# Recurrent attention and two expert layers: one matrix-engine visit per later attention unit, new planner costs and due times, weights converted in pairs

## The chip, the cores and the metric

The kernel runs on one core of one Trainium2 chip. The metric is the device time of one launch in microseconds: 944.38 us as the median of three runs (943.25 to 944.75). One further run was profiled.

## What is computed

The reference applies a linear recurrence to r, k, v, w (4 batches, 8 heads, 768 tokens, 48 dimensions a head) and puts its output, 3072 tokens of 384 values, through two layers of two products each:

```python
for t in range(S):                                   # per batch and head
    cur = einsum('bhd,bhe->bhde', u[None] * kt, vt)
    y[:, :, t] = einsum('bhd,bhde->bhe', rt, state + cur)
    state = wt[:, :, :, None] * state + einsum('bhd,bhe->bhde', kt, vt)
h = x @ w_in                                         # 384 x 2048
x = (max(h, 0) + alpha * min(h, 0)) @ w_out          # 2048 x 384
h = x @ w_in2
out = (h * clip(h + 3, 0, 6) / 6) @ w_out2
```

## The kernel before

**Attention units.** The tokens are cut into 12 thirds of 256 tokens (three a batch); each has four pairs of heads. One third and one pair is a unit: 48 units, n = 0 to 47, each of two chunks of 128 tokens. The decay products come from two scans on DVE (`scan_t`, L386, from the back; `scan_g`, L402, from the front), between them a floor (L394) and a reciprocal (L399) on two columns. `scaled` (L423) multiplies k and r by these factors and writes `kr`, on DVE or POOL. On PE a unit then has three pieces:

- `pa` (L477, L484): k times r into bank A, and transposes of k into the same bank;
- `kv` (L516, L520): the products of the transposed k (`kT`, copied by ACT, L509) with v, into the second half of bank A, from which DVE makes the state (`Y`, L560, L562) and ACT its scaled copy (`sbd`, L538);
- `pc` (L588 to L599): the output y from state and from X, the masked `pa` (ACT writes its diagonal, L458, from a sum over the token products of L332 and L339; DVE copies the triangle in, L499).

ACT and DVE split y into a high and a low part of reduced format (L635, L641). For the fourth pair of a third they go by six small DMAs into the rows where the layers expect them (L651).

**Slots.** A layer is computed for blocks of 512 tokens (j = 0 to 5) and pieces of 128 hidden channels (f = 0 to 15): slot s = 96 m + 16 j + f for layer m. In a slot PE makes `h` (nine matmuls of 128x512, three for each of three input pieces: high by high, high by low, low by high, L765 to L767), ACT and DVE make the gate (`q` L801 or L803, `pg` L808 or L812) and split it into `g` (high L818, low L821, DVE or POOL), and PE adds nine more matmuls into three accumulators, `acc`. Blocks 0 to 5 need the outputs of units 8j to 8j+7, so units run ahead of slots; from unit 8 on they stand between slots.

**Weights** come as 64-bit numbers and are converted on the chip, one (f, part) of 128x384 at a time: ACT takes bits (`rest`, L95), DVE joins them and sets the sign (L98, L103), ACT writes the high part (L738), DVE or POOL the low one (L742). All 32 of layer 0 are made while the first 16 slots run, those of layer 1 in the slots around 96.

**Order.** Each step is given to `Plan` with its durations by engine (`where`), a due time in slots, what it needs and which buffers it takes. `Plan.run` replays this on paper: again and again it takes the engine that can start first, on it the ready step of the lowest due time, and where two engines can do a step, the one that comes first. DVE steps marked `pair` and all POOL steps exclude each other on paper. The order that comes out is written into the program, so on the chip every engine works through its list as it stands. While no `h` has begun, idle time of PE on paper is filled with small `warm` matmuls (L682).

**Checks.** Range checks (`fall`, `sum_w`, `chw` are their columns) run beside all this and set a flag at the end; by it the program goes on to a general path or not. The trace holds no instruction of that path.

**Visits.** From unit 16 on (`FUSE`), PE does `pc` of unit n-1 and `kv` of unit n in one step: `add_output` is put into `waiting` and is called when `kv` of the next unit is planned. `pa` of unit n is a step of its own.

## Time and profile before

| | |
|---|---|
| median of three runs | 944.38 us |
| profiled run, time | 943.6 us |
| profiled run, span from first to last instruction | 941.8 us |
| PE busy | 920.7 us (98%) |
| PE weight loads busy | 744.6 us (79%) |
| DVE busy | 557.1 us (59%) |
| ACT busy | 532.2 us (57%) |
| POOL busy | 133.8 us (14%) |
| granted TensorE clock, mean | 0.995 |

Busy time counts an engine from the start of an instruction to its end. On PE matmuls overlap, so that a row of 0.39 us follows the row ahead of it after 0.23 us: what a matmul costs is read from start to start, and the same goes for short instructions in a row on DVE. Times below are microseconds from the start of the span. Lines are those of the kernel before.

### The profile page before, as it was taken

The page shows a single profiled execution, that of the slowest core. Times are in us where ns is not written, and L with a number is a line of the kernel's source. Part 1 is how long each engine was busy: PE and PEld are TensorE (multiplying, and loading weights), DVE is VectorE, ACT ScalarE, POOL GpSimd, SP SyncE. Part 2 cuts the span into 40 slices and gives each one's busy share as a digit, 9 for nine tenths or more (in the row PEclk, how much of TensorE's full clock was granted, in tenths as well). Part 3 has the DMA queues.
Part 4 walks back from the last instruction along what each step waited for, and adds up shares of the span by engine and source line. Part 5 has one row for each costly group of instructions (what it writes and reads, how often), then busy time and mean ns, then how long its engine had stood idle before and what let it go on. Part 6 is the DMA issues. An engine that isn't in the chain of part 4 may idle for free.

```text
span 941.8 us, 13747 instructions
## 1 busy us (share of the span) xinstructions
PE 920.7 (98%) x4914; PEld 744.6 (79%) x4914; DVE 557.1 (59%) x1087; ACT 532.2 (57%) x1267; POOL 133.8 (14%) x132
## 2 busy tenths in 40 slices
PE   7899999999999999999999999999999999999997
PEld 5677777887888788878888888888888888888885
DVE  8999997555655645564369897353353443443432
ACT  5888777555655655565368886363353353443331
POOL 4333244021111201100012130000000000000000
PEclk9999999999999999999999999999999999999999
DMA  8888314122321320110056630060150330410001
GB/s 249 245 263 280 100 55 145 55 66 72 116 67 55 103 64 31 55 64 9 9 174 194 185 118 1 1 201 1 29 173 1 96 106 1 155 47 1 34 1 37
DMA packets 36750, 86.20 MB, mean 92 GB/s; under 512 B 5056, under 2 KB 7488, under 8 KB 36672
## 3 DMA queue, kind: packets, MB, share of 16 engines
q1 hardware_dynamic: 36240, 84.44, 28.5%
q8 instruction: 41, 0.67, 0.3%
q10 hardware_dynamic: 432, 0.79, 0.2%
q14 instruction: 37, 0.30, 0.1%
HBM read 73.41 MB, written 9.44 MB: 88 GB/s over the span
## 4 chain that ended last, share of the span: by engine, by line
PE 85%; DVE 4%; issue 2%; ACT 1%; POOL 1%; DVEq 0%; POOLq 0%; ACTq 0%
PE acc L765 14%; PE acc L766 13%; PE acc L767 13%; PE h L765 13%; PE h L767 13%; PE h L766 13%; PE A L477 2%; PE y L595 2%; PE y L588 1%; PE A L484 1%; DVE wb L98 1%; DVE wb L103 1%; DVE w L742 1%; DVE pg L808 0%; POOL kr L423 0%
## 5 line engine op out<-in xcount | busy, mean ns | idle before, releaser
L765 PE MATMUL acc<-g,w 128*128 128x512 f32 x576 | 228.9, 397 | 0.0
L767 PE MATMUL acc<-g,w 128*128 128x512 f32 x576 | 224.6, 390 | 0.0
L766 PE MATMUL acc<-g,w 128*128 128x512 f32 x576 | 224.4, 390 | 0.0
L818 ACT ACTIVATE g<-pg 128x512 fp32r<-128x512 f32 x192 | 120.7, 629 | 139.6 <-PE acc L767 126.6
L821 DVE TENSOR_TENSOR g<-pg,g 128x512 fp32r<-128x512 f32 x176 | 122.4, 696 | 124.6 <-ACT g L818 124.3
L765 PEld LDWEIGHTS acc<-g,w 128*128 128x128 f32 x576 | 108.1, 188 | 23.4 <-issue 0.4
L767 PEld LDWEIGHTS acc<-g,w 128*128 128x128 f32 x576 | 108.1, 188 | 22.8
L766 PEld LDWEIGHTS acc<-g,w 128*128 128x128 f32 x576 | 108.2, 188 | 21.2
L812 DVE SCALAR_TENSOR_TENSOR pg<-q,h 128x512 f32<-128x512 f32 x96 | 65.9, 687 | 99.6 <-ACT q L803 99.4
L803 ACT ACTIVATE q<-h,three 128x512 f32<-128x512 f32 x96 | 65.7, 685 | 101.9 <-PE h L767 101.7
L808 DVE SCALAR_TENSOR_TENSOR pg<-h,q 128x512 f32<-128x512 f32 x96 | 66.0, 688 | 96.1 <-ACT q L801 96.1
L765 PE MATMUL h<-xt,w 128*128 128x512 f32 x288 | 116.1, 403 | 0.8 <-ACT w L738 0.7
L767 PE MATMUL h<-xt,w 128*128 128x512 f32 x288 | 113.0, 392 | 0.7 <-DVE w L742 0.7
L766 PE MATMUL h<-xt,w 128*128 128x512 f32 x288 | 112.2, 390 | 0.0
L765 PE MATMUL h<-x,w 128*128 128x512 f32 x288 | 112.0, 389 | 0.0
L766 PE MATMUL h<-x,w 128*128 128x512 f32 x288 | 112.0, 389 | 0.0
L767 PE MATMUL h<-x,w 128*128 128x512 f32 x288 | 112.0, 389 | 0.0
L801 ACT ACTIVATE q<-h,nal 128x512 f32<-128x512 f32 x96 | 65.5, 683 | 74.0 <-PE h L767 71.8
L423 POOL TENSOR_TENSOR kr<-un,tg 112x512 f32<-112x512 f32 (+1 forms) x43 | 46.4, 1080 | 230.2 <-PE y L588 207.0
L767 PEld LDWEIGHTS h<-xt,w 128*128 128x128 f32 x288 | 54.1, 188 | 13.9 <-DVE w L742 2.0
L765 PEld LDWEIGHTS h<-xt,w 128*128 128x128 f32 x288 | 54.9, 191 | 12.4 <-ACT w L738 1.4
L765 PEld LDWEIGHTS h<-x,w 128*128 128x128 f32 x288 | 54.1, 188 | 11.3
(95 smaller groups left out, 1264.8 us busy)
## 6 DMA issues: line engine op xcount, KB each, us to landing
wraw<-in_w SPq DMA_DIRECT2D x64, 384.0 KB, 4.1
un<-in_unit SPq DMA_DIRECT2D x48, 337.3 KB, 3.2
raw<-in_w SPq DMA_DIRECT2D x32, 384.0 KB, 3.9
rk<-in_tok SPq DMA_DIRECT2D x24, 384.0 KB, 3.8
v<-in_vch SPq DMA_DIRECT2D x12, 384.0 KB, 3.1
x2d<-st SPq DMA_DIRECT2D x18, 256.0 KB, 2.1
x2r<-x2d SPq DMA_DIRECT2D x18, 256.0 KB, 4.7
out<-st SPq DMA_DIRECT2D x15, 256.0 KB, 4.5
```

Of the source, the lines that this page charges most:

```text
L423: eng[e].tensor_tensor(out=u["kr"][:, i].rearrange("p a (c s) -> p a c s", c=2), in0=u["in"][:, 0 : 2 * TH].rearrange("p (a c s) -> p a c ...
L477: nc.tensor.matmul(A[h][:, cs], kr[r0 : r0 + D, 0, cs], kr[r0 : r0 + D, 1, cs], start=True, stop=True,)
L595: nc.tensor.matmul(y[0:m0, cs], v[:, c, c0 : c0 + m0], X[:, c, :], start=False, stop=True, skip_group_check=True,)
L765: nc.tensor.matmul(ps, whi, xhi, start=start, stop=False, skip_group_check=True)
L766: nc.tensor.matmul(ps, whi, xlo, start=False, stop=False, skip_group_check=True)
L767: nc.tensor.matmul(ps, wlo, xhi, start=False, stop=stop, skip_group_check=True)
L801: nc.scalar.activation(q, k["h"], AF.Relu, scale=nal[:, f : f + 1])
L803: nc.scalar.activation(q, k["h"], AF.Relu, bias=three)
L808: nc.vector.scalar_tensor_tensor(out=p, in0=k["h"], scalar=0.0, in1=k["q"], op0=ALU.max, op1=ALU.subtract)
L812: nc.vector.scalar_tensor_tensor(out=p, in0=k["q"], scalar=6.0, in1=k["h"], op0=ALU.min, op1=ALU.mult)
L818: nc.scalar.activation(k["g"][:, 0], k["p"], AF.Copy)
L821: eng[e].tensor_tensor(out=k["g"][:, 1], in0=k["p"], in1=k["g"][:, 0].bitcast(F32), op=ALU.subtract)
```

## The change

Six things change together.

1. For units 16 to 47 (`late`) one PE step, `add_visit`, does `pc` of unit n-1, `kv` of unit n and `pa` of unit n+1. KV moves from bank A into the second half of y's bank. `triangle` waits for `pa` and no longer for `kv`. `kT` has one buffer and `kr` three (two before).
2. The floor is gone: the reciprocal reads the scan's column, and ACT copies that column for the check at the end (`keep`). There is one `gfirst`, not two.
3. Weights are converted in groups (f, 0) and (f-2, 1): 14 pairs and four single ones for each layer. A pair is loaded by two DMAs, and `rest`, `join`, sign, high and low each work on 768 columns. The low part of a pair is on DVE alone.
4. The planner gets new durations for nearly every step, waits by engine, a model of SP's queue, and of two engines that can start at the same moment takes the one that could have started first by itself (`asked`), which bears on POOL and DVE.
5. A table, `URGENCY`, shifts due times of 23 kinds of steps in four ranges of due time up to slot 95, and ties some kinds to one engine: token products (`weigh_tokens`) and the halves of `kr` of the first units (`scale_half`) to POOL in the first range, the low part of g (`add_slot.glo`) to DVE up to slot 80.
6. `v` buffers take the place of `wv` for the range check of weights.

Of the table some lines, and the planner's constants, where they are read, and the choice between engines:

```diff
+URGENCY = {
...
+    "add_slot.glo": {1: (0, "DVE"), 2: (0, "DVE")},
+    "add_slot.h_": {1: (-3.0, None), 2: (1.0, None), 3: (-1.0, None)},
...
+    "scale_half": {0: (0, "POOL")},
+    "second": {2: (-0.5, None), 3: (2.0, None)},
+    "state1": {1: (7.5, None)},
+    "weigh_tokens": {0: (0, "POOL"), 1: (1.0, "DVE"), 2: (0, "DVE")},
...
-    LATENCY = 0.08
-    SAME = {"PE": 0.0, "DVE": 0.1, "ACT": 0.15, "POOL": 0.1, "SP": 0.0}
-    SPARE = 0.46
-    COLD = 9.5
-    LOCK = True
-    BEGIN = {"PE": 1.2, "DVE": 2.0, "ACT": 2.0, "POOL": 3.0, "SP": 0.6}
+
+    TAIL = {"PE": 0.0, "DVE": 0.08, "ACT": 0.1, "POOL": 0.04, "SP": 0.0}
+    LATENCY = {"PE": 0.26, "DVE": 0.06, "ACT": 0.05, "POOL": 0.08, "SP": 0.0}
+    SAME = {"PE": 0.0, "DVE": 0.02, "ACT": 0.02, "POOL": 0.02, "SP": 0.0}
+    STAGES = (-0.5, 16, 80, 95)
+    ISSUE, FLIGHT = 0.45, 1.6
+    SPARE = 0
+    COLD = 8.0
+    BEGIN = {"PE": 1.4, "DVE": 3.1, "ACT": 5.2, "POOL": 3.0, "SP": 0.7}
```

```diff
+        kind = kind or fn.__qualname__.replace("<locals>.", "").split(".", 1)[1]
+        if due < self.STAGES[-1]:
+            stage = sum(due >= x for x in self.STAGES)
+            shift, engine = URGENCY.get(kind, {}).get(stage, (0.0, None))
+            due += shift
+            if engine and len(where) > 1:
+                where = {engine: where[engine]}
```

```diff
             for e, lst in ready.items():
                 if lst:
                     t = min(earliest(e, o) for o in lst)
-                    if best is None or t < best[0]:
-                        best = (t, e)
+                    o = min((o for o in lst if earliest(e, o) <= t), key=lambda o: rank(e, o))
+                    asked = max(free[e], o["t"][e])
+                    if best is None or (t, asked) < best[:2]:
+                        best = (t, asked, e, o)
```

```diff
+            t, _, e, o = best
...
             o["eng"], o["start"], o["end"] = e, t, t + d
-            free[e] = t + d
-            if self.LOCK and (e == "POOL" or (e == "DVE" and o["pair"])):
-                pair = t + d
+            free[e] = t + d - self.TAIL[e]
+            if e == "POOL" or (e == "DVE" and o["pair"]):
+                pair = free[e]
             if e == "SP":
-                o["end"] = t + d + 2.0
+                queue = o["end"] = max(t + self.ISSUE + self.FLIGHT, queue) + d
+                free[e] = max(t + self.ISSUE, queue - self.FLIGHT - d)
             if not (o.get("filler") and self.started):
```

Units: the floor and its columns, then `pa` and `kv`:

```diff
-        def floor(e):
-            nc.vector.tensor_scalar(
-                fall[0:PR, n], u["T"][:, :, 0], 2.0**-60, None, op0=ALU.max
-            )
-
         def recip(e):
-            nc.vector.reciprocal(first_g[:, :, 0], fall[0:PR, n])
+            nc.vector.reciprocal(first_g[:, :, 0], u["T"][:, :, 0])
+
+        def keep(e):
+            nc.scalar.activation(fall[0:PR, n], u["T"][:, :, 0], AF.Copy)
...
-        first_g = gfirst[n % 2]
-        gb = plan.buf("gfirst", 2)
-        o_t = plan.op({"DVE": 0.34}, d - 3.7, scan_t, [o_load], new=[tgb], use=[ub_], pair=True)
-        o_f = plan.op({"DVE": 0.07}, d - 2.4, floor, [o_t], use=[tgb])
-        o_d1 = plan.op({"DVE": 0.08}, d - 2, recip, [o_f], new=[gb])
+        first_g = gfirst
+        gb = plan.buf("gfirst", 1)
+        o_t = plan.op({"DVE": 0.69}, d - 3.7, scan_t, [o_load], new=[tgb], use=[ub_], pair=True)
+        o_d1 = plan.op({"DVE": 0.16}, d - 2.4, recip, [o_t], new=[gb], use=[tgb])
+        plan.op({"ACT": 0.2}, d + 2, keep, [o_t], use=[tgb])
         o_g = plan.op(
-            {"DVE": 0.34}, d - 1.5, scan_g, [o_d1], use=[tgb, ub_, gb], pair=True
+            {"DVE": 0.69}, d - 1.5, scan_g, [o_d1], use=[tgb, ub_, gb], pair=True
```

```diff
-        o_pa = plan.op({"PE": 0.89 + 0.1 * nkv}, d - 2, pa, o_kr, new=abufs, use=[krb])
+        pa_us = 0.73 + 0.1 * nkv
+        if waiting:
+            o_pa = waiting.pop()(pa_us, pa, o_kr, abufs, [krb])
+        else:
+            o_pa = plan.op({"PE": pa_us}, d - 2, pa, o_kr, new=abufs, use=[krb])
...
-        ktb = plan.buf("kT", 2)
+        ktb = plan.buf("kT", 1)
...
+        kv_after = [o_kt, v_op[t][0]]
+        if late:
+            o_tri = plan.op({"DVE": 0.73}, d - 1.5, triangle, [o_pa, o_x], use=abufs + [xb])
         else:
-            o_kv = plan.op({"PE": 0.1 + 0.13 * nkv}, d + 0.4, kv, kv_after, use=kv_use)
-        o_tri = plan.op({"DVE": 0.61}, d - 1.5, triangle, [o_kv, o_x], use=abufs + [xb])
```

```diff
+        def add_visit(more=0.0, then=None, after=(), new=(), use=()):
+
+
+            yb = plan.buf("y", 1)
+            last_pc, last_us, last_need, last_use, last_out = u["prev"]
+
+            def run(e):
+                bank = room(e)
+                if last_pc:
+                    last_pc(e, bank)
+                u["KV"] = bank[:, 1, 0 : 2 * D].rearrange("p (c e) -> p c e", c=2)
+                kv(e)
+                if then:
+                    then(e)
+
+            o = plan.op(
+                {"PE": last_us + 0.13 * nkv + more}, d + 0.4, run,
+                kv_after + last_need + list(after), new=[yb] + list(new),
+                use=[ktb, vb] + last_use + list(use), kind="visit",
+            )
+            add_states(o, [yb])
+            if last_out:
+                last_out(o, yb)
+            ended.append((pc, pc_us, need, [krb, xb, vb] + sb, add_output))
+            return o
...
+        if late:
+            u["prev"] = ended.pop()
+            if n + 1 < NU:
+                waiting.append(add_visit)
+            else:
+                add_visit()
+                ended.pop()
+                add_end()
         else:
-            add_output()
+            add_states(o_kv, abufs)
```

Weights:

```diff
         def load(e):
-            k["raw"] = wp.tile([P, DM], w1.dtype, tag=tag, name=f"wraw{name}")
-            nc.sync.dma_start(k["raw"], (w1, w2)[m][f, part])
+            k["raw"] = wp.tile([P, n, DM], w1.dtype, tag=tag, name=f"wraw{name}")
+            for i, (m, f, part) in enumerate(keys):
+                nc.sync.dma_start(k["raw"][:, i], (w1, w2)[m][f, part])
...
+        o_l = plan.op({"SP": 1.26 * n}, due - 4, load, new=[wb])
+        o = plan.op({"ACT": 0.18 + 0.45 * n}, due - 0.2, rest, [o_l], new=[ab, bb], use=[wb])
         for i in (1, 2):
             o = plan.op(
-                {"DVE": 0.47}, due - 2, lambda e, i=i: k["steps"][i](), [o], use=[wb, ab, bb],
-                pair=True,
-            )
-        read = [add_range(key, due, o_l, [wb], lambda: k["raw"])] if m else []
-        o = plan.op({"ACT": 0.42}, due - 2.5, hi, [o] + read, use=[wb, bb])
-        w_ops[key] = plan.op(
-            {"POOL": 0.96, "DVE": 0.47}, due - 1, lo, [o], use=[bb, wb], pair=True
-        )
+                {"DVE": 0.15 + 0.4 * n}, due - 2, lambda e, i=i: k["steps"][i](), [o],
+                use=[wb, ab, bb], pair=True,
+                kind="join",
+            )
...
+        o = plan.op({"ACT": 0.21 + 0.31 * n}, due - 2.5, hi, [o] + read, use=[wb, bb])
+        where = {"POOL": 1.05, "DVE": 0.55} if n == 1 else {"DVE": 0.15 + 0.4 * n}
+        o = plan.op(where, due - 1, lo, [o], use=[bb, wb], pair=True)
...
-    for s, part, f in halves:
-        add_weight((0, f, part), s + W0)
+    for s in range(NF + 2):
+        add_weights([(0, f, part) for s1, part, f in halves if s1 == s], s + W0)
```

**PE, slots 39 to 41.** y, A and kr with a number are tiles of that unit, h and g of that slot; first before, the visit with the output of unit 29 and KV of unit 30 behind h of slot 40:

```order
L599 MATMUL y29_3143<-X29_2967,v7_2551 48x128
L516 MATMUL A30_3091<-v7_2551,kT30_3114 64x48
L520 MATMUL A30_3091<-v7_2551,kT30_3114 48x48
L516 MATMUL A30_3091<-v7_2551,kT30_3114 64x48
L520 MATMUL A30_3091<-v7_2551,kT30_3114 48x48
L765 MATMUL acc0_2_0_2856<-g38_3043,w0_6_1_1323 128x512
```

Further down in the same list, behind nine acc matmuls, comes `pa` of unit 31:

```order
L766 MATMUL acc0_2_2_2878<-g38_3043,w0_6_1_1323 128x512
L767 MATMUL acc0_2_2_2878<-g38_3043,w0_6_1_1323 128x512
L477 MATMUL A31_3188<-kr31_3162 128x128 x4
L484 MATMUL A31_3188<-ident_90,kr31_3162 128x112 x2
L765 MATMUL h42_3206<-xt2_1846,w0_10_0_1457 128x512
L766 MATMUL h42_3206<-xt2_1846,w0_10_0_1457 128x512
```

After, the same place (KV of unit 30 goes into y30 here):

```order
L651 MATMUL y30_3119<-X29_2962,v7_2533 48x128
L655 MATMUL y30_3119<-X29_2962,v7_2533 48x128
L565 MATMUL y30_3119<-v7_2533,kT30_3048 64x48
L569 MATMUL y30_3119<-v7_2533,kT30_3048 48x48
L565 MATMUL y30_3119<-v7_2533,kT30_3048 64x48
L569 MATMUL y30_3119<-v7_2533,kT30_3048 48x48
L519 MATMUL A31_3130<-kr31_3082 128x128 x4
L527 MATMUL A31_3130<-ident_93,kr31_3082 128x112 x2
L871 MATMUL acc0_2_0_2772<-g39_3095,w0_9_0_1372 128x512
L872 MATMUL acc0_2_0_2772<-g39_3095,w0_9_0_1372 128x512
L873 MATMUL acc0_2_0_2772<-g39_3095,w0_9_0_1372 128x512
L871 MATMUL h41_3150<-xt2_1905,w0_9_0_1372 128x512
```

`pa` of unit 31 has moved from between acc and h to right behind `kv` of unit 30, and the acc matmuls of slot 39 now stand around h of slot 41, two slots behind their own.

**DVE, weights of f = 6 in the first layer** (wb is joined, then signed; w its low part; tg a scan). Before:

```order
L808 SCALAR_TENSOR_TENSOR pg4_1156<-h4_1037,q4_1069 128x512
L98 SCALAR_TENSOR_TENSOR wb0_6_0_1120<-wraw0_6_0_888,wa1_107 128x384
L98 SCALAR_TENSOR_TENSOR wb0_4_1_1151<-wraw0_4_1_909,wa0_106 128x384
L103 SCALAR_TENSOR_TENSOR wb0_6_0_1120<-wraw0_6_0_888,wb0_6_0_1120 128x384
L103 SCALAR_TENSOR_TENSOR wb0_4_1_1151<-wraw0_4_1_909,wb0_4_1_1151 128x384
L386 SCALAR_TENSOR_TENSOR tg0_111<-un14_1008,restart_108 112x258
L402 SCALAR_TENSOR_TENSOR tg1_112<-un13_922,gfirst1_110 112x258
L742 TENSOR_TENSOR w0_6_0_1178<-wb0_6_0_1120,w0_6_0_1178 128x384
L742 TENSOR_TENSOR w0_4_1_1182<-wb0_4_1_1151,w0_4_1_1182 128x384
```

After:

```order
L98 SCALAR_TENSOR_TENSOR wb0_6_0_1118<-wraw0_6_0_667,wa0_109 128x768
L928 TENSOR_TENSOR g2_1157<-pg2_1135,g2_1157 128x512
L103 SCALAR_TENSOR_TENSOR wb0_6_0_1118<-wraw0_6_0_667,wb0_6_0_1118 128x768
L430 SCALAR_TENSOR_TENSOR tg0_113<-un14_1070,restart_111 112x258
L438 RECIPROCAL gfirst_112<-tg1_114 112x2
L915 SCALAR_TENSOR_TENSOR pg3_1191<-h3_1050,q3_1079 128x512
L843 TENSOR_TENSOR w0_6_0_1182<-wb0_6_0_1118,w0_6_0_1182 128x2x384
L444 SCALAR_TENSOR_TENSOR tg1_114<-un13_989,gfirst_112 112x258
L98 SCALAR_TENSOR_TENSOR wb0_7_0_1133<-wraw0_7_0_920,wa0_109 128x768
```

Two instructions of 384 columns became one of 768, and the low part of g stands on DVE between them.

**POOL, first units** (kr halves of 112x256, rk the token products). Before:

```order
L423 TENSOR_TENSOR kr0_167<-un0_142,tg_0_162 112x256
L332 TENSOR_TENSOR rk1_158<-rk1_158 128x384
L423 TENSOR_TENSOR kr1_221<-un1_181,tg_1_209 112x256 x2
L423 TENSOR_TENSOR kr2_271<-un2_197,tg_2_239 112x256
L423 TENSOR_TENSOR kr3_298<-un3_200,tg_3_262 112x256
L332 TENSOR_TENSOR rk2_207<-rk2_207,u_sb_95 128x384
L332 TENSOR_TENSOR rk3_229<-rk3_229,u_sb_95 128x384
L296 TENSOR_SCALAR nal_96<-alp_61 128x16
```

After:

```order
L465 TENSOR_TENSOR kr0_170<-un0_143,tg_0_164 112x256 x2
L375 TENSOR_TENSOR rk0_153<-rk0_153 128x384
L375 TENSOR_TENSOR rk0_153<-rk0_153,u_sb_98 128x384
L375 TENSOR_TENSOR rk1_173<-rk1_173 128x384
L375 TENSOR_TENSOR rk1_173<-rk1_173,u_sb_98 128x384
L465 TENSOR_TENSOR kr1_255<-un1_179,tg_1_219 112x256 x2
L465 TENSOR_TENSOR kr2_303<-un2_190,tg_2_269 112x256 x2
L338 TENSOR_SCALAR nal_99<-alp_61 128x16
L465 TENSOR_TENSOR kr3_340<-un3_217,tg_3_324 112x256
```

All four products of a third, and both halves of `kr`, are now POOL's.

## Rows read from the trace of the kernel before

**Rows 1.** The page: span and count of instructions

```profile
span 941.8 us, 13747 instructions
```

**Rows 2.** Windows: us, then busy us (instructions) of each engine, clock, DMA

```profile
0.00:55.58 55.58, 44.60 (x419) 33.34 (x420) 50.07 (x130) 41.35 (x139) 22.20 (x36) 0.94 0.79 234
55.58:141.10 85.52, 82.59 (x477) 62.52 (x478) 83.77 (x173) 69.57 (x182) 27.67 (x21) 1.00 0.56 176
150.73:941.80 791.07, 784.89 (x3959) 642.08 (x3958) 414.76 (x769) 413.47 (x927) 79.41 (x71) 1.00 0.23 72
```

**Rows 3.** Waits of PE, 150.73 to the end: heading, and no row under it

```profile
engine line waited for: us in total, times, longest us
```

**Rows 4.** Waits of PE over the span: us, times, longest; one of ten rows

```profile
PE A L477 <- DVE fall L394: 1.0, 1, 1.0
```

**Rows 5.** Timeline of DVE: start us, us, instruction; gate of the sixteenth slot

```profile
140.43 0.68 DVE L808 SCALAR_TENSOR_TENSOR pg<-h,q 128x512 f32<-128x512 f32 x1
```

**Rows 6.** Timeline of PE: first h matmul, and a steady pair of slots

```profile
55.58 0.47 PE L765 MATMUL h<-xt,w 128*128 128x512 f32 x1
...
154.94 0.39 PE L765 MATMUL h<-xt,w 128*128 128x512 f32 x1
...
156.98 0.60 PE L588 MATMUL y<-kr,sbd 112*112 112x128 f32 x4
...
157.99 0.21 PE L516 MATMUL A<-v,kT 128*64 128x48 f32 x1
...
158.30 0.50 PE L765 MATMUL acc<-g,w 128*128 128x512 f32 x1
...
160.57 0.71 PE L477 MATMUL A<-kr 48*128 48x128 f32 x8
...
161.30 0.47 PE L765 MATMUL h<-xt,w 128*128 128x512 f32 x1
...
163.47 0.39 PE L765 MATMUL acc<-g,w 128*128 128x512 f32 x1
```

**Rows 7.** Timeline of PE: kv, then pa, in the first stretch

```profile
32.65 0.21 PE L516 MATMUL A<-v,kT 128*64 128x48 f32 x1
...
32.96 0.71 PE L477 MATMUL A<-kr 48*128 48x128 f32 x8
```

**Rows 8.** Timeline of DVE: consecutive instructions, for the prices

```profile
134.45 0.68 DVE L808 SCALAR_TENSOR_TENSOR pg<-h,q 128x512 f32<-128x512 f32 x1
135.06 0.15 DVE L399 RECIPROCAL gfirst<-fall 112x2 f32<-112x2 f32 x1
135.13 1.00 DVE L98 SCALAR_TENSOR_TENSOR wb<-wraw,wa 128x384 int32<-128x384 int32 x2
136.05 1.01 DVE L103 SCALAR_TENSOR_TENSOR wb<-wraw,wb 128x384 int32<-128x384 int32 x2
136.99 0.68 DVE L402 TENSOR_TENSOR_SCAN tg<-un,gfirst 112x258 f32<-112x258 f32 x1
137.60 0.66 DVE L821 TENSOR_TENSOR g<-pg,g 128x512 fp32r<-128x512 f32 x1
138.18 0.25 DVE L562 SCALAR_TENSOR_TENSOR Y<-Y,tg,A 112x48 f32<-112x48 f32 x1
```

**Rows 9.** Timeline of POOL, then of DVE: one POOL product and the floor

```profile
4.99 0.64 POOL L423 TENSOR_TENSOR kr<-un,tg 112x256 f32<-112x256 f32 x1 [1.93 <-DVE tg L386]
7.92 0.99 POOL L332 TENSOR_TENSOR rk<-rk 128x384 f32<-128x384 f32 x1 [2.30 <-DMA rk<-in_tok]
...
84.74 1.29 POOL L332 TENSOR_TENSOR rk<-rk 128x384 f32<-128x384 f32 x1 [7.09 <-DMA rk<-in_tok]
...
85.05 1.00 DVE L394 TENSOR_SCALAR fall<-tg 112x2 f32<-112x2 f32 x1
```

**Rows 10.** Timeline of PE, then DVE: end of h, low half of g

```profile
303.86 0.40 PE L767 MATMUL h<-xt,w 128*128 128x512 f32 x1
...
308.67 0.67 DVE L821 TENSOR_TENSOR g<-pg,g 128x512 fp32r<-128x512 f32 x1
```

266 lines of the change are left out of this document (155 added, 111 removed).

## The prediction

> **What bounds the kernel now.** I read the windows first, then the waits of PE, then PE's own order of time. The span of 941.8 us [rows 1] falls into three stretches [rows 2]: before the first `h` matmul at 55.58 us [rows 6], from there to 141.1, and the rest. In the last stretch (150.73 to the end, 791 us) the list of PE's waits is empty [rows 3]: PE alone sets its length, DVE is busy for 415 of 791 us, and whatever is to be gained there must be time of PE itself. The middle stretch is another matter. DVE is busy for 83.8 of 85.5 us [rows 2], and PE's longest wait behind it is for a DVE instruction [rows 4]. The gate of the sixteenth slot (the last `pg` that needs a first-layer weight to be new) ends at 141.1 [rows 5]; DVE was busy for 50.1 + 83.8 = 133.9 us up to it. So up to slot 16 DVE's queue decides, behind it PE's.
>
> PE in a steady pair of slots [rows 6]: an undisturbed block of nine matmuls takes 156.98 - 154.94 = 2.04 us, 0.227 each. The visit "output of unit n-1, then KV of unit n" takes 158.30 - 156.98 = 1.32; the acc block behind it and ahead of the next visit takes 160.57 - 158.30 = 2.27; `pa` takes 0.73, and the h block behind it 163.47 - 161.30 = 2.17. So the way out of `pa` costs 0.13, and the acc block's 0.23 is the way out of one visit and the way into the next; I split it into halves.
>
> **The change, part by part.** *One visit, not two.* The matmuls stay the same: `pc`, `kv` and `pa` now stand in a row, and one way in and one way out go. Of 0.23 + 0.13 = 0.36 a unit the joined visit keeps one way out, 0.13; saved is 0.23 us, if going from `kv` to `pa` costs nothing of its own. The trace has that pair in the first stretch: `kv` starts at 32.65 and `pa` at 32.96 [rows 7], 0.31 us for eight passes, the same as from `kv` to `acc` (157.99 to 158.30). The longest stretch holds 28 `pa` visits (of 48 units; one stands about every 10.4 us until 444 us), and all 28 are now behind a `kv`: 28 x 0.23 = **6.4 us**. Bounds: 28 x 0.12 = 3.4 if the way into `pa` (0.11) stays, 31 x 0.23 = 7.1 if three earlier units count too. No cover is needed, since PE waits for nothing there; what is late next is PE again.
>
> What the rule of the tiling page makes of it: the Trainium skill, TensorEngine Tiling (Array Packing), section Key Properties, says that changing the tiling mode, not just the tile, drains the TensorE. `kv` and `pa` split the array differently, so by that rule the way from one to the other would be paid inside the visit too, and the saving would be 3.4 and not 6.4. The 0.31 us of the early pair speaks against a charge on top of the one that every exit from `kv` pays.
>
> Moved with it: the KV tile lies in the output's bank, so the copies of state wait for the whole visit, and `triangle` waits for `pa` alone. `pa` of unit n+1 comes a fraction of a slot earlier than its own visit did; its `kr` on POOL must be ready, or output and KV behind it in PE's queue wait too. POOL is busy for 79 of 791 us in this stretch [rows 2], so I cost this at nothing; if the cover failed, each 0.1 us would cost 3 us over the units.
>
> *Up to slot 16: DVE's work.* Prices are start to start from consecutive instructions [rows 8]: a 2-element op 0.07 (reciprocal at 135.06, next at 135.13), a 512-element op 0.61 and 0.58 (at 134.45 and 137.60), a 384-element op 0.46 (two from 135.13 to 136.05), a scan 0.61. A 768-element op is in no row: it lies between 0.61 and two of 0.46, and the line through 0.46 and 0.595 gives 0.46 + 3 x 0.135 = 0.87 as an estimate, which I take; a 256-element op by the same line 0.33. Counted in the order of DVE up to the sixteenth gate, before against after: join and sign 64 x 0.46 = 29.4 against 28 x 0.87 + 8 x 0.46 = 28.0, so -1.4; low halves of weights 22 x 0.46 against 14 x 0.87, +2.1 (eight fewer on POOL); low halves of g 8 against 15, +4.2 (none on POOL now); `kr` 7 whole and 5 halves against 1 whole, -5.3; floors 19 against none, -1.3; scans 38 against 36, -1.2; one token product and one memset less, -0.8; state, triangle and output copies that now come later, -1.9. Sum: **-5.6 us**. Pairing thus gives little; the rest is work moved.
>
> *The port.* An op on POOL stops DVE: the product at 84.74 took POOL 1.29, and the floor, a 2-element op, that DVE started at 85.05 ended only at 86.05, after 1.00 us [rows 9]. In the first 141 us POOL is busy for 22.2 + 27.7 = 49.9 us [rows 2], and DVE for 133.9; counted with the prices above DVE's work is some 117, so about 17 us are stretch, a third of a us for each of POOL. After, POOL has 6 to 12 us less to do by that place (41 against 43 products, the 512-element ones of `g` gone, more of the cheap half `kr`). That is -2 to -4 us; I take -2.8.
>
> So the sixteenth gate ends at 141.1 - 5.6 - 2.8 = 132.7. Not all of 8.4 is a gain: in the new order PE has by then one slot of acc matmuls (2.04) and one unit (about 2.4) fewer behind it: 8.4 - 4.5 = 3.9. The stall of 1.0 behind it [rows 4] should go as well: 5. Upper bound: all of PE's stall. Between 55.58 and 150.73 PE has 33 blocks of 2.04, nine `pa` and eight or nine of the other visit at the prices above (18.1, with 3.1 for entries), 88.5 of 95.15, so 6.7 us are stall; and DVE's work before the first gate is 5.1 us less by the same prices (ten token products and `kr` pieces are POOL's now), so the first `h` can come up to 5.1 earlier: 11.8 together. Lower bound: nothing, see the second rival. I take **7.0 us**, near the 5 of the DVE sum, and above it because the planner's durations now stand near the rows (scan 0.69, low half of `kr` on POOL 0.64), so that fewer DVE instructions should stand in line behind a POOL one.
>
> *The rest.* The weights of a pair come by two DMAs in a row, the same bytes, with the DMA engines 56% busy in the middle stretch [rows 2]: nothing. Between the last output of block 1 and the `h` that needs it stand 27 matmuls, `kv` and `pa`, 7.3 us, for output copies and six small DMAs; if these took longer, PE would wait once, a us or so, at slot 16 alone (in later blocks slots stand between): nothing in the sum. `keep` puts a 2-element copy per unit on ACT, which has half its time free behind 150 us and is not what the sixteenth gate waits for: nothing, or at worst 0.2 x 17 units = 3 us of ACT in the crowded stretch. The second layer's weights are made between 480 and 600 us; PE did not wait for them [rows 3], and DVE's work there changes by about +3 us (POOL's low halves) with POOL's stretch gone: nothing. The last store is untouched.
>
> **Sum.** The profiled run took 943.6 us for a span of 941.8, and the median of the three is 944.38, 0.8 above it. 6.4 + 7.0 = 13.4 less: span 928.4, run 930.2, against the median **931.0 us**.
>
> **Rivals.** *The start gains nothing (0.15).* POOL takes all token products and `kr` halves before the first `h`: 33 products instead of 22 up to `kr` of unit 11, about 26 us instead of 17 at 0.64 and 0.99 for a half `kr` and a product [rows 9]. If the port is what decides, those 9 us eat the 5.1 of DVE and the gate comes no earlier. For it: rows 9; against: in the first stretch POOL was busy for only 22 of 55.6 us. Then 944.4 - 6.4 = 938.0. The Trainium skill, SBUF — State Buffer, section Who interferes with whom, has the rule behind this: a DVE instruction with two SBUF inputs and a GpSimd one that reads SBUF exclude each other for the whole instruction. The stretched floor agrees.
>
> *The way into `pa` is still paid (0.10).* 6.4 becomes 3.4: 934.0.
>
> *DVE stops being the bound at once (0.12).* All 11.8 us come: 944.4 - 6.4 - 11.8 = 926.2, or 925.5 with 31 units.
>
> *Slower: second-layer input too late (0.05).* In the new order the acc matmuls of a slot begin two slots after its `h` block in slots 16 to 80, not three: between the end of `h` and the first acc stand one visit (2.2 us) and 24 matmuls (5.4 us), 7.6 us in all. A `g` took 303.86 + 0.40 = 304.26 to 308.67 + 0.67 = 309.34, 5.1 us [rows 10]. Up to 7.6 nothing is lost; beyond it each us costs 1 us in each of 32 pairs. At 8.05 us the 13.4 are gone; at 8.5 they are overdrawn, 931 + 32 x 0.9 = 960. Against it: DVE and ACT are about half busy there.
>
> *The joined visit does not arise (0.02):* the order shows that it does. The same time within 1.9 us, 0.2% (what a measurement of this kernel can tell from no change), would need both gains to fail.
>
> **How the numbers follow.** Forecast 0.56: 931, between 926 and 936. With the rivals: start without gain 0.15 at 938, way in paid 0.10 at 934, full gain 0.12 at 926, slower 0.05, same 0.02. For 8 in 10 the range is 924.5 to 938.5. Faster 0.93, same 0.02, slower 0.05.
>
> **What would show it.** Right: from slot 20 to 80 one visit a unit, 0.31 us from `kv` to `pa`, no second 2.17 us block, and PE's wait list empty from the seventeenth slot on; the sixteenth gate near 133 us; DVE still above 90% up to there. Wrong: `pa` starting later than 0.31 us behind `kv`; the first `h` behind 56 us with POOL back to back (second rival's sign); waits of acc blocks for `g` between 150 and 470 us.

## The result, and the profile after

| | before | changed |
|---|---|---|
| median of six runs each | 943.82 us | 935.32 us (933.76 to 939.31) |
| ratio | | 0.9914 (95%: 0.9895 to 0.9934) |
| profiled run, span | 941.8 us | 937.5 us |
| first `h` | 55.58 | 55.97 |
| gate of the sixteenth slot ends | 141.1 | 135.63 |

The kernel became 8.5 us faster by the medians; 13.4 had been forecast (931.0 us). The profiled run of the changed kernel is the slowest of its six (939.31), so its trace shows less of a gain than the medians do; below a second profile of it stands beside this one. Lines are those of the kernel whose trace is shown; the experiments' lines may be shifted by a few.

The page of the changed kernel: span, then busy us, share and instructions of each engine.

```profile
span 937.5 us, 13798 instructions
...
PE 919.5 (98%) x4999; PEld 753.4 (80%) x4999; DVE 553.0 (59%) x957; ACT 528.8 (56%) x1260; POOL 139.2 (15%) x128
```

Windows of the changed kernel (us, then busy us and instructions of PE, PEld, DVE, ACT and POOL, granted clock, DMA share, GB/s): up to the first `h`, from there to the sixteenth gate, and 2.5 us close behind a wait that is told of below.

```profile
0.00:55.97 55.97, 49.98 (x508) 39.00 (x509) 45.63 (x103) 43.27 (x153) 31.58 (x47) 1.00 0.82 241
55.97:135.63 79.66, 77.07 (x441) 58.72 (x439) 76.76 (x128) 62.59 (x142) 11.20 (x9) 1.00 0.55 176
151.97:154.51 2.54, 2.54 (x7) 1.97 (x6) 2.47 (x6) 1.84 (x6) 0.04 (x1) 0.51 0.01 3
```

These answer to [rows 2]. Up to the sixteenth gate DVE is now busy for 45.6 + 76.8 = 122.4 us, against 133.9 before, and POOL for 42.8 against 49.9. DVE's list got 11.5 us lighter, and the gate only 5.5 us earlier: DVE stood idle for 13.2 us on the way, against 7.3. The gate's row, on DVE:

```profile
134.94 0.69 DVE L915 SCALAR_TENSOR_TENSOR pg<-h,q 128x512 f32<-128x512 f32 x1
```

Waits of PE over the whole span (us, times, longest):

```profile
engine line waited for: us in total, times, longest us
PE acc L872 <- DVE g L928: 2.5, 1, 2.5
PE A L519 <- POOL kr L465: 2.2, 2, 1.2
PE h L871 <- DVE pg L915: 2.0, 2, 1.7
PE warm L772 <- POOL ident L318: 1.4, 1, 1.4
PE y L644 <- ACT sbd L589: 1.0, 2, 0.7
PE A L565 <- ACT kT L558: 1.0, 2, 0.5
PE y L651 <- DVE X L548: 0.7, 1, 0.7
```

None of them lies behind 160 us. The largest is new: PE waits for a low half of `g`, once, for 2.5 us.

A steady visit, timeline of PE: `pc` (y from kr and sbd), `kv` (y from v), `pa` (A from kr), then h and acc.

```profile
163.57 0.60 PE L644 MATMUL y<-kr,sbd 112*112 112x128 f32 x4
...
164.58 0.21 PE L565 MATMUL y<-v,kT 128*64 128x48 f32 x1
...
164.89 0.72 PE L519 MATMUL A<-kr 48*128 48x128 f32 x8
...
165.62 0.47 PE L871 MATMUL h<-xt,w 128*128 128x512 f32 x1
...
167.75 0.39 PE L871 MATMUL acc<-g,w 128*128 128x512 f32 x1
```

`kv` to `pa` is 164.89 - 164.58 = 0.31 us, as in [rows 7]. The h block behind the visit takes 167.75 - 165.62 = 2.13, where before two blocks a unit were over 2.04, with 2.27 and 2.17 [rows 6].

**One table for all runs.** The work of PE from slot 24 to slot 80, and from there to the end, is the same in every kernel here, and PE waits for nothing in it (but for one 0.46 us in `pa_apart`). So each trace splits at two places: the start of `h` of slot 24 and of slot 80. In all but `before`, `visits_alone`, `no_table` and `only_glo`, PE has done 12 acc matmuls more by slot 24 (22 1/3 blocks, not 21); 12 x 0.227 = 2.72 us are taken off there and added behind. The two rows of PE, before, then changed (186.08 - 2.72 = 183.36):

```profile
182.16 0.48 PE L765 MATMUL h<-xt,w 128*128 128x512 f32 x1
...
472.02 0.39 PE L765 MATMUL h<-xt,w 128*128 128x512 f32 x1
```

```profile
186.08 0.39 PE L871 MATMUL h<-xt,w 128*128 128x512 f32 x1
...
466.92 0.39 PE L871 MATMUL h<-xt,w 128*128 128x512 f32 x1
```

| kernel | median, us | first h | h of slot 24 | from there to slot 80 |
|---|---|---|---|---|
| before | 943.8 to 944.7 | 55.58 | 182.16 | 289.86 |
| changed | 935.32 | 55.97 | 183.36 | 283.56 |
| changed, second profile | 936.51 | 54.58 | 179.56 | 283.56 |
| visits_alone | 940.39 | 54.37 | 184.15 | 284.17 |
| pa_apart | 940.30 | 52.71 | 177.28 | 290.17 |
| rk_slow | 932.36 | 56.80 | 180.83 | 283.56 |
| flight4 | 933.26 | 58.09 | 177.85 | 283.56 |
| load_late | 939.46 | 54.05 | 184.67 | 283.56 |
| rk_scale | 936.38 | 55.48 | 182.19 | 283.56 |
| single_dve | 936.43 | 52.01 | 180.43 | 283.56 |
| rk_scan | 937.12 | 56.04 | 181.65 | 283.56 |
| dma_more | 937.26 | 56.67 | 181.15 | 283.55 |
| no_table | 944.06 | 52.24 | 188.57 | 283.56 |
| only_glo | 940.36 | 52.85 | 186.25 | 283.56 |

Read it by columns. The last one has two values: about 290 with two visits a unit, about 283.6 with one. Between the two slots stand 25 `pa` visits in the kernel before and none of its own in the changed one; this gains 289.86 - 283.56 = 6.30 us, 0.25 each (5.7 us in `visits_alone`). All else is the column of slot 24, which comes from one execution each (those times move by up to 4 us between executions of one kernel), and the medians. In the changed kernel's first profile the start lost 1.2 us, and the last store landed 0.8 us later behind its last matmul: 6.3 - 1.2 - 0.8 = 4.3, the difference of the two spans. Medians of two changed kernels are compared with care: each stands beside its own runs of the kernel before, each ratio is known to some 2 us either way, and the changed kernel itself gave 935.32 and 936.51. Differences of 3 to 5 us between two of them are at the edge of what this tells, and their sizes are rough.

### The profile page after: what moved, and what is told of

Its sections match the earlier page's. It is cut to its first block, busy times and chain, and to the rows that moved or that the text cites. A ratio compares the mean times of both kernels' runs of the same rounds, so it can differ in the third digit from the quotient of the medians.

```text
span 937.5 us, 13798 instructions
## 1 busy us (share of the span) xinstructions
PE 919.5 (98%) x4999; PEld 753.4 (80%) x4999; DVE 553.0 (59%) x957; ACT 528.8 (56%) x1260; POOL 139.2 (15%) x128
## 4 chain that ended last, share of the span: by engine, by line
PE 90%; DVE 3%; DMA 2%; ACT 2%; issue 1%; POOL 0%; SPq 0%; ACTq 0%; DVEq 0%; POOLq 0%
PE acc L871 14%; PE h L871 14%; PE acc L872 14%; PE acc L873 14%; PE h L873 13%; PE h L872 13%; PE A L519 3%; PE y L651 2%; DMA un<-in_unit 2%; PE y L644 2%; PE A L527 1%; DMA rk<-in_tok 1%; DVE tg L444 1%; ACT wa L95 1%; PE y L655 1%
## 5 line engine op out<-in xcount | busy, mean ns | idle before, releaser
L928 DVE TENSOR_TENSOR g<-pg,g 128x512 fp32r<-128x512 f32 x162 | 112.6, 696 | 116.5 <-ACT g L925 114.8
L465 POOL TENSOR_TENSOR kr<-un,tg 112x512 f32<-112x512 f32 (+1 forms) x55 | 55.6, 1012 | 344.9 <-DVE tg L444 266.9
L871 PEld LDWEIGHTS h<-xt,w 128*128 128x128 f32 x288 | 54.5, 189 | 15.4 <-issue 2.9
L873 PEld LDWEIGHTS h<-xt,w 128*128 128x128 f32 x288 | 54.4, 189 | 11.5
L872 PEld LDWEIGHTS h<-xt,w 128*128 128x128 f32 x288 | 54.4, 189 | 11.3
```

Source lines behind the costliest of these rows:

```text
L465: eng[e].tensor_tensor(out=u["kr"][:, i].rearrange("p a (c s) -> p a c s", c=2), in0=u["in"][:, 0 : 2 * TH].rearrange("p (a c s) -> p a c ...
L871: nc.tensor.matmul(ps, whi, xhi, start=start, stop=False, skip_group_check=True)
L872: nc.tensor.matmul(ps, whi, xlo, start=False, stop=False, skip_group_check=True)
L873: nc.tensor.matmul(ps, wlo, xhi, start=False, stop=stop, skip_group_check=True)
L928: eng[e].tensor_tensor(out=k["g"][:, 1], in0=k["p"], in1=k["g"][:, 0].bitcast(F32), op=ALU.subtract)
```

## The experiments

**Visits undone, and visits alone.** In `pa_apart` the changed kernel plans `pa` by itself:

```diff
-        if waiting:
-            o_pa = waiting.pop()(pa_us, pa, o_kr, abufs, [krb])
-        else:
-            o_pa = plan.op({"PE": pa_us}, d - 2, pa, o_kr, new=abufs, use=[krb])
+        o_pa = plan.op({"PE": pa_us}, d - 2, pa, o_kr, new=abufs, use=[krb])
...
-            if n + 1 < NU:
-                waiting.append(add_visit)
-            else:
-                add_visit()
+            add_visit()
+            if n + 1 == NU:
                 ended.pop()
```

> The changed kernel with one edit: pa of a unit is a PE step of its own again (output of unit n-1 and KV of unit n stay joined, KV stays in y's bank). Theory A (the joined visit gives what the steady rows show: the excess of the acc and h blocks over 2.04 us fell from 9.8 us for 28 units to 3.2 us for 30, about 0.245 us a unit): 28 x 0.245 = 6.9 us come back, 935.3 becomes 942 (941 to 943.5). Rival (the way into pa is still paid, 0.12 a unit): 3.4 us, 938.7. Rival (most of the gain is from the start): within 2 us of 935.3.

Measured 940.30 us (0.9963 of before, 0.9944 to 0.9981): 5.0 more than the changed kernel. This is less than the 6.9 us of the theory (941 to 943.5), and the median alone lies between it and the first rival. The steady stretch grew by 6.6 us, near what was expected; the start of this profile was the earliest of all, and its list has no wait for `g` at slot 16.

`visits_alone` puts the whole of part 1 into the kernel before, and nothing else. Of its edit, the place where `kv` is planned:

```diff
...
-        kv_after, kv_use = [o_kt, v_op[t][0]], abufs + [ktb, vb]
-        if waiting:
-            o_kv = waiting.pop()(d + 0.4, 0.13 * nkv, kv, kv_after, kv_use)
+        kv_after = [o_kt, v_op[t][0]]
+        if late:
+            o_tri = plan.op({"DVE": 0.61}, d - 1.5, triangle, [o_pa, o_x], use=abufs + [xb])
...
```

> The kernel before with part 1 of the change alone (joined visits from unit 16 on, KV in y's bank, triangle behind pa, kr of three buffers); planner constants, weights, floor and due times as before. Theory A: 943.8 - 6.9 = 937 (936 to 938.5), with no waits of PE behind 150 us beyond what the kernel before shows. Rival (way into pa still paid): 940.4. Rival (the visits pay only with the new due times, because pa or g comes late in the old order): 941 to 946, with rows A <- kr or acc <- g in PE's waits between 150 and 470 us.

Measured 940.39 us (0.9959, 0.9945 to 0.9974), a gain of 3.7, where 6.9 had been expected and 3.4 stood for a way into `pa` that is still paid. The median alone would have told for that rival. The table tells otherwise: 5.7 us came in the steady stretch, and 2.0 were lost before slot 24. Timeline of PE, where they went, then of the DVE instruction that it waits for and of POOL beside it:

```profile
137.82 0.49 PE L811 MATMUL acc<-g,w 128*128 128x512 f32 x1 [0.43 <-ACT g L864]
141.28 0.50 PE L812 MATMUL acc<-g,w 128*128 128x512 f32 x1 [2.96 <-DVE g L867]
...
142.71 0.63 PE L600 MATMUL y<-kr,sbd 112*112 112x128 f32 x2
```

```profile
139.65 1.58 DVE L867 TENSOR_TENSOR g<-pg,g 128x512 fp32r<-128x512 f32 x1
```

```profile
139.42 1.26 POOL L423 TENSOR_TENSOR kr<-un,tg 112x512 f32<-112x512 f32 x1 [1.09 <-issue]
```

PE waits 2.96 us for a low half of `g`. DVE, without a gap before it, makes that half in 1.58 us, beside a `kr` of POOL; alone it takes 0.66 [rows 8]. From 142.71 to 144.50 the granted clock is 0.50. So the joined visit is worth what its rows say, and DVE's list took a part of it back near slot 16, here as in the changed kernel, though by another instruction.

**The stall of slot 16.** In the changed kernel DVE's list stands at a load. Timeline of DVE (rk the token products, pg a gate, g its low half), then of PE:

```profile
145.45 0.56 DVE L375 TENSOR_TENSOR rk<-rk 128x384 f32<-128x384 f32 x1 [3.20 <-DMA rk<-in_tok]
...
146.52 0.68 DVE L915 SCALAR_TENSOR_TENSOR pg<-h,q 128x512 f32<-128x512 f32 x1
149.78 0.56 DVE L375 TENSOR_TENSOR rk<-rk 128x384 f32<-128x384 f32 x1 [2.58 <-DMA rk<-in_tok]
150.25 0.68 DVE L928 TENSOR_TENSOR g<-pg,g 128x512 fp32r<-128x512 f32 x1
```

```profile
148.11 0.39 PE L871 MATMUL acc<-g,w 128*128 128x512 f32 x1
150.99 0.75 PE L872 MATMUL acc<-g,w 128*128 128x512 f32 x1 [2.49 <-DVE g L928]
...
151.97 0.63 PE L871 MATMUL h<-xt,w 128*128 128x512 f32 x1
...
155.21 0.39 PE L871 MATMUL acc<-g,w 128*128 128x512 f32 x1
```

The product at 149.78 waits 2.58 us for its tokens; the low half of `g` of slot 16, ready since 147.9, stands behind it; PE's acc matmul at 150.99 waits 2.49 us for it. The chain of waits has that load for 6.83 us, issued among three stores of the first layer's output. Then the next h block takes 155.21 - 151.97 = 3.24 us, not 2.04: the third window above has a granted clock of 0.51 there, the lower level. The stall costs 2.5 + 1.2 = 3.7 us. `rk_slow` tells the planner that these loads land later:

```diff
                 queue = o["end"] = max(t + self.ISSUE + self.FLIGHT, queue) + d
                 free[e] = max(t + self.ISSUE, queue - self.FLIGHT - d)
+                if o["kind"] == "add_third.load_rk" and t > 100:
+                    o["end"] += 4.0
```

> The changed kernel, with the planner told that the token loads of the thirds behind 100 us land 4 us later on paper, near the 6.8 us of the trace; so on DVE the products of thirds 6 and up stand behind the low half of g of slot 16, not ahead of it. Theory A (DVE stands in line behind a DMA: the product waits 2.58 us for its tokens at 149.78, g16 comes at 150.93 and PE waits 2.5 us; the h block behind it then takes 3.24 us at a granted clock below full): the wait goes and that block takes 2.04 to 2.2, 3.5 us less in the profile, 1 to 3.5 in the median. Rival B (the start is limited by what DVE and POOL have to do, so PE waits as long elsewhere): within 1 us of 935.3, and another wait of 2 to 3 us in PE's list at 145 to 165 us.

Measured 932.36 us (0.9872, 0.985 to 0.9894), 3.0 less than the changed kernel (the two intervals just miss each other), and the wait is gone from the trace: theory A. (Its profiled run is the slowest of four.) The same two places, DVE and PE:

```profile
148.05 0.69 DVE L930 TENSOR_TENSOR g<-pg,g 128x512 fp32r<-128x512 f32 x1 [0.70 <-PE A L529]
...
149.09 0.56 DVE L377 TENSOR_TENSOR rk<-rk 128x384 f32<-128x384 f32 x1
...
150.07 0.55 DVE L377 TENSOR_TENSOR rk<-rk,u_sb 128x384 f32<-128x384 f32 x1
```

```profile
149.96 0.39 PE L873 MATMUL acc<-g,w 128*128 128x512 f32 x1
...
150.64 0.39 PE L873 MATMUL h<-xt,w 128*128 128x512 f32 x1
...
152.68 0.39 PE L873 MATMUL acc<-g,w 128*128 128x512 f32 x1
```

The low half of `g` now stands ahead of the products and waits for none of them; PE goes through, and the h block behind takes 2.04.

**The changed kernel again**, without an edit:

> The changed kernel, unchanged, for a second profile: its profiled run of 939.3 is the slowest of six (the fastest 933.8). Theory (transfers are the part that differs from run to run: the same order up to the first h gave it at 55.97, 56.80 and 52.71 us in three profiles): a first h at 52 to 57 us, the wait for g at slot 16 of 1.5 to 3 us in every run, and a span that follows the first h, near 937.5 - (55.97 - first h) within 1 us. Rival (the wait at slot 16 is the part that differs): the first h at 55 to 57 again and a wait shorter by as much as the span.

Its four timed runs have a median of 936.51 us (933.14 to 939.48). The second profile's span is 933.5 us, where the theory, from the first `h` alone, gives 936.1. DVE and PE at the stall:

```profile
147.55 0.56 DVE L375 TENSOR_TENSOR rk<-rk 128x384 f32<-128x384 f32 x1 [1.79 <-DMA rk<-in_tok]
148.03 0.68 DVE L928 TENSOR_TENSOR g<-pg,g 128x512 fp32r<-128x512 f32 x1
```

```profile
146.87 0.39 PE L871 MATMUL acc<-g,w 128*128 128x512 f32 x1
148.77 0.50 PE L872 MATMUL acc<-g,w 128*128 128x512 f32 x1 [1.51 <-DVE g L928]
...
149.34 0.40 PE L871 MATMUL h<-xt,w 128*128 128x512 f32 x1
...
151.42 0.39 PE L871 MATMUL acc<-g,w 128*128 128x512 f32 x1
```

The wait is 1.51 us, and the block behind it takes 2.08 at full clock. Of 4.0 us between the two spans, 1.4 are the first `h`, 1.0 the wait, 1.2 the clock behind it and 0.3 the last store. Both theories hold a part: the loads land at other times from run to run, and this shows at both places.

**Transfers and the start.** The first `h` needs six small DMAs of block 0. Those issued between 44 and 54 us (first and last issue, then times from issue to landing), before, then changed:

```profile
L651 SPq DMA_DIRECT2D xt<-x x6: 586/592/957, 48.7 to 52.3; - x6
...
DMA to landing us min/median/max: 2.0/2.0/3.2
```

```profile
L696 SPq DMA_DIRECT2D xt<-x x6: 585/586/597, 46.9 to 52.1; - x6
...
DMA to landing us min/median/max: 3.0/6.2/7.4
```

The median says little of the first `h`, which comes 0.8 to 1.3 us behind the landing of the last of the six, before as in the changed kernel: the last took 2.0 us before (52.3 + 2.0 = 54.3) and 3.0 in the changed kernel (52.1 + 3.0 = 55.1). So a delay of one us can be theirs. In the second profile the median is 4.0, in `pa_apart` 3.7 and in `rk_slow` 4.6, with the same order on every engine up to the first `h`.

`load_late` holds the weights back:

```diff
-    "add_weights.load": {0: (1.0, None), 1: (-2.5, None)},
+    "add_weights.load": {0: (4.0, None), 1: (-2.5, None)},
```

> The changed kernel with one number: due time of the loads of weights in the first range +4 slots, not +1, so that eight weight loads and not ten are issued ahead of the six small DMAs of the first block's output (as in the kernel before). Theory A (the first h at 55.97 waits for those DMAs, which take 6.2 us to land in the median, against 2.0 before, behind weight transfers): they land in 2 to 4 us, the first h starts at 52.5 to 54.5, and the time is 1 to 2 us less, less where weights then come late. Rival B (POOL and DVE set the first h, DMAs do not): first h at 55.5 to 56.5, time the same within 1 us. Rival C (the weights are needed that early): first h earlier, but PE waits for w within the first slots, time the same or up to 3 us more.

Measured 939.46 us (0.9947, 0.9931 to 0.9964), 4.1 slower: rival C by the sign, and more than the 3 us it allowed. The small DMAs landed in 3.6 us and the first `h` began at 54.05, but the third `h` only at 66.83, against 62.18. Between the first and the third PE waits 1.2 us for X and 1.3 for `kT`, not for weights, and from 63.98 to 66.83 the granted clock is 0.50: the loss is shown, the reason that rival C gave for it is not. `dma_more` adds three transfers to `rk_slow`:

```diff
...
                 nc.sync.dma_start(k["raw"][:, i], (w1, w2)[m][f, part])
+                if m == 0 and part == 0 and f in (2, 6, 3):
+                    nc.sync.dma_start(spare, w1[f, part])
```

> The kernel of rk_slow (932.4, its first h at 56.80) with three more transfers of 384 KB each (a weight from HBM to a spare place in HBM, read by nobody) in the first 45 us, at the loads of weights 2, 6 and 3. Theory C (from 34 to 50 us the DMA engines are full, and the first h waits for the small DMAs of block 0 and for a unit behind them): 3 x 384 KB at 0.25 to 0.4 MB a us is 3 to 4.6 us, first h at 59 to 62, time 934.5 to 937. Theory A (DVE's and ACT's work sets the first h and transfers are hidden): first h at 56 to 57.5, time within 1 us of 932.4.

Measured 937.26 us (0.9923, 0.9904 to 0.9942; four runs of 936.4 to 939.1), 4.9 more than `rk_slow`. The price is near that of theory C, but the profiled run, the fastest of the four, has its first `h` at 56.67 and slot 24 at 181.15, as `rk_slow` has. So the medians tell that more transfers cost time, and no trace here shows where. `rk_scan` is `rk_slow` with a unit's check on ACT behind its second scan, so that ACT's list stands at no load:

```diff
-        plan.op({"ACT": 0.51}, d + 1, check, [o_load], use=[ub_])
+        plan.op({"ACT": 0.51}, d + 1, check, [o_load, o_g], use=[ub_])
```

> The kernel of rk_slow (932.4) with the range check of a unit on ACT behind the unit's second scan, not behind its load, so that ACT's list never stands at a load (1.8 us ahead of the first h in the profile of the changed kernel). Theory (transfers set the first h through two waits, ACT's for a unit and that of the h for the small DMAs; only the first goes): 0 to 2 us less, 930.5 to 932.5. Rival (ACT's wait is the one that sets it): 2 to 3 us less, first h at 51 to 53. Rival (the new order of ACT's steps costs): 933 to 936.

Measured 937.12 us (0.9916, 0.9894 to 0.9938), 4.8 more than `rk_slow` and above even the last rival's 933 to 936: the new order costs. ACT no longer waited for a unit, and the first `h` stood at 56.04: without ACT's wait, 1.8 us in the changed kernel's first profile, it came no earlier. `flight4` gives all loads a longer flight on paper:

```diff
-    ISSUE, FLIGHT = 0.45, 1.6
+    ISSUE, FLIGHT = 0.45, 4.0
```

> The changed kernel with one planner constant: flight of a DMA 4.0 us on paper, not 1.6, for all loads, near the 5 to 8 us from issue to landing that the trace has in the first 60 us. Theory A (what the planner has wrong is the landing of loads, and every engine's list has instructions standing in line behind one): PE's wait for g at slot 16 goes as in rk_slow, ACT no longer waits 1.8 us for a unit before the first h; 929.5 to 933. Rival (the longer paper times push loads and first h back): first h at 57 or later, 934 to 938.

Measured 933.26 us (0.987, 0.9852 to 0.9888). Its waits of PE:

```profile
engine line waited for: us in total, times, longest us
PE warm L772 <- POOL ident L318: 1.4, 1, 1.4
PE h L871 <- DVE pg L915: 0.7, 1, 0.7
```

Besides the 1.4 us ahead of the first matmul PE waits once, for 0.7 us: with landing times near the trace's, the planner's order has PE hardly ever wait, though its first `h` came at 58.09, 5.8 us behind the landing of the last small DMA, so that here something else set it. It is as fast as `rk_slow`, within both intervals; these two are the fastest kernels here.

**What the table is worth.** `no_table` empties it:

```diff
-URGENCY = {
...
-}
+URGENCY = {}
```

> The changed kernel with an empty table of due-time shifts and ties; visits, weights in pairs, planner durations and floor as changed. Theory A (the rest of the change, apart from the visits' 6.3 to 6.9 us, gave 2 us at the start, and the table made both the gain, by moving work off DVE, and the 3 us stall of slot 16, by tying token products to DVE): without it the stall goes (products may run on POOL) and DVE's gain goes: 936 to 939. Rival (the table gives most of what the start gained): 939 to 943. Rival (the table only costs): 931 to 934.

Measured 944.06 us (0.9993, 0.9979 to 1.0006): above even the first rival's 939 to 943. The whole gain is gone, though the steady stretch kept its 6.3 us: the start is 6.4 us later at slot 24. POOL has the low halves of `g` there (busy groups of POOL, then of DVE, 55 to 150 us: busy us, mean ns of one, idle before):

```profile
L904 POOL TENSOR_TENSOR g<-pg,g 128x512 fp32r<-128x512 f32 x16 | 26.3, 1649 | 13.3 <-ACT g L901 11.4 <-PE y L631 1.9
```

```profile
L98 DVE SCALAR_TENSOR_TENSOR wb<-wraw,wa 128x768 int32<-128x768 int32 x12 | 14.5, 1218 | 2.9 <-ACT wa L95 2.9
```

`only_glo` gives the table that one tie back:

```diff
-URGENCY = {}
+URGENCY = {
+    "add_slot.glo": {1: (0, "DVE"), 2: (0, "DVE")},
+}
```

> The kernel of no_table (944.06) with one entry of the table back: the low half of g on DVE up to slot 80. In no_table POOL takes the low halves of g of all of the first 17 slots (26.3 us busy from 55 to 150 us, 1.65 us each) and DVE's 768-element joins take 1.22 us, not 0.99 as with the table; its slot 24 comes 6.4 us later than before, which eats the visits' 6.3. Theory (the port: POOL's 512-element instructions hold DVE, and this tie is what the table is worth): most of the 8.7 us comes back, 936 to 939. Rival (the shifts of due times are what it is worth, as they set which step stands ahead): 941 to 944.

Measured 940.36 us (0.9941, 0.992 to 0.9962): 3.7 of 8.7 us back, between the theories (by the two ratios, 0.9993 and 0.9941, 4.9). DVE's join takes 1013 ns again:

```profile
L98 DVE SCALAR_TENSOR_TENSOR wb<-wraw,wa 128x768 int32<-128x768 int32 x12 | 12.2, 1013 | 0.0
```

So POOL's 512-element instructions on `g`, and DVE's stretch beside them, are part of what the table avoids; the other 4 to 5 us are in its remaining entries and weren't taken apart. Nor do these runs tell how much of the 3.7 is the stretch on DVE and how much the longer time of POOL itself, 1649 ns against 0.68 us on DVE, for each low half. `rk_scale` undoes, in `rk_slow`, the ties of the first units' products and `kr` halves to POOL:

```diff
-    "scale_half": {0: (0, "POOL")},
...
-    "weigh_tokens": {0: (0, "POOL"), 1: (1.0, "DVE"), 2: (0, "DVE")},
+    "weigh_tokens": {1: (1.0, "DVE"), 2: (0, "DVE")},
```

> The kernel of rk_slow (932.4) with the first range's ties to POOL undone: token products and halves of kr of the first units may run on DVE or POOL again. Theory A (DVE's work is what the start is made of; the ties took about 5 us of it away before the first h): first h 1 to 4 us later with DVE over 95% busy before it, time 933.5 to 937. Rival B (POOL and the port set the start): first h earlier, time 929 to 932. Rival C (transfers set the first h): first h within 1 us of 53 to 57 us as in the runs so far, time within 1 us of 932.4.

Measured 936.38 us (0.9904, 0.9887 to 0.9921), 4.0 more: these ties seem to gain (the two intervals, 0.9887 to 0.9921 and 0.985 to 0.9894, just overlap), though the first `h` is not later (55.48); the loss shows between there and slot 24.

**Pairs.** `single_dve` converts one weight at a time in both layers, in `rk_slow`; the low halves of what were pairs stay on DVE. The first layer's edit:

```diff
...
-        add_weights([(0, f, part) for s1, part, f in halves if s1 == s], s + W0)
+        for key in [(0, f, part) for s1, part, f in halves if s1 == s]:
+            add_weights([key], s + W0)
...
```

> The kernel of rk_slow (932.4) with weights converted one (f, part) at a time, the low half of what were pairs still on DVE alone: 28 x 3 instructions of 384 columns in place of 14 x 3 of 768 in each layer. By the rows (0.46 against 0.86 start to start) that is 14 x 3 x 0.06 = 2.5 us more of DVE up to slot 16: theory (pairing is worth its saved instructions): 933 to 936. Rival (pairing is worth nothing, or costs, since a pair waits for its second load, not needed for two more slots): 930 to 932.5. Rival (it is worth far more, by ACT and the waits between engines): over 937.

Measured 936.43 us (0.992, 0.9896 to 0.9943), 4.1 more, above the 933 to 936 of the theory, where the rows of DVE had given 2.5.

## Why the prediction was right, and where it missed

- **The range** (924.5 to 938.5) and the sign held; the size was 8.5 us and not 13.4, and the term that missed is the start: slot 24 came 1.2 us later in the first profile and 2.6 earlier in the second, where 7.0 had been forecast. That the time still fell inside the range is the visits' doing and in part luck: the range had room for a start that gives nothing.
- **The visits, 6.4 us: right, and a little low.** 0.25 a visit, against 0.23: 6.3 us for 25 visits behind slot 24 (5.7 in `visits_alone`). For the 28 of the prediction that would be 7.1, as an estimate. `kv` to `pa` stayed at 0.31, so the rival "the way into `pa` is still paid" fell, with its 3.4. The rule of the Trainium skill, TensorEngine Tiling (Array Packing), section Key Properties, that a change of tiling mode drains the TensorE, would have had that price; no row here shows one on top of the 0.31.
- **DVE's work: the direction right, the step from it to the gate wrong.** 8.4 us less of DVE had been counted, and 11.5 were measured. But the prediction moved the gate by all of it, as if DVE stayed the bound throughout. It came 5.5 us earlier (6.7 in the second profile): the lighter list waited 6 us more for others.
- **The start's 7.0 us: the term that was mis-sized.** 5.5 at the gate, less the 4.5 us of PE's work left over, plus the old stall of 1.0, is 2.0; then the new stall of slot 16 took 3.7. That is -1.7, and the profile has -1.2. In the medians the start gave 8.5 - 6.3 = 2.2, and without the stall (`rk_slow`) 11.7 - 6.3 = 5.4 us. Six of the joined visits stand ahead of slot 24, some 1.5 us by the price above (an estimate), so that 3.9 is left for the start itself, below the 5 of the DVE sum; the raise from 5 to 7.0 had no ground.
- **"PE would wait once, a us or so, at slot 16 alone: nothing in the sum": the step that failed.** It did wait there, for 1.5 and 2.5 us, and not for the output's small DMAs: the token products, tied to DVE, stood at a load, and `g` behind them. On POOL such a wait had cost DVE nothing that shows: 7.09 us in [rows 9], with DVE busy for 83.8 of the 85.5 us around it. It was not the tie alone: before, DVE had two products here as well, at 145.25 and 146.31, and waited for no load; and `rk_slow` keeps the tie and changes the place in the list. The order shows the products ahead of the low half of `g`; the working counted their busy time and not who queues behind them. One of the prediction's signs of being wrong, a wait of an acc block for `g` behind 150 us, thus came, once, at 150.99.
- **"The weights of a pair by two DMAs: nothing": open.** In the first profile the small DMAs ahead of the first `h` took 6.2 us to land in the median, not 2.0, with ten weight loads issued ahead of them, not eight. But the last of them, 3.0 us against 2.0, can have held the first `h` by one us at most, other executions of that order have 3.7 to 4.6, and `single_dve`, with ten ahead too, has 2.6. Later loads cost more than they gave.
- **"Pairing gives little": low.** 4.1 us by its undoing, rough as that size is, against the counted 1.4 of joins and signs.
- **"The start gains nothing, by the port": not so in this kernel**, since undoing POOL's ties made it slower, not faster. But without the table, with `g` on POOL, the start lost 6.4 us, more than that rival has it lose. The rule behind it (the Trainium skill, SBUF — State Buffer, section Who interferes with whom: a GpSimd instruction that reads SBUF and a DVE one with two SBUF inputs lock each other out) agrees with the joins of 1218 ns beside POOL's 16 low halves and 1013 without them. The floor, which the prediction set beside that rule, has one SBUF input (`fall<-tg`), so that its 1.00 us is not a case of it.
- **"Second-layer input too late" between slots 16 and 80:** no wait of PE behind 160 us; it fell.

**Open:** what of the other entries of the table gives the remaining 4 to 5 us; what the floor's removal, the new durations and the `v` buffers give by themselves, as no run undid them one by one; and what sets the first `h` in each run (52.7 to 56.8 us in four profiles with the same order of every engine up to it): of these 4.1 us, 2.6 are there when the last small DMA is issued, at 49.75 to 52.33.

## What to carry to other kernels

Before moving an instruction to a busy engine with a fixed list, ask what it waits for, not only how long it takes: a wait for a load that cost nothing on an idle engine stops everything behind it on the busy one. Split a trace at places of equal work; a gain that is there in one stretch and lost in another shows as two numbers, where the median shows neither. A planner's table is worth what its paper times are worth: landing times near the traced ones gave the same gain by one constant.
